# Moving the last chunk of batch 0 ahead of the second mean, at the start of a linear-attention and ELU-MLP kernel

## Chip, cores, metric

The kernel runs on one core of a Trainium2 chip. The metric is the device time of one execution, in microseconds, as the median over several executions of the same kernel.

## The reference

The work is a linear attention without softmax, a root-mean-square norm of each head's output, and a two-layer MLP with an ELU between the layers:

```python
# q, k, v: (8 batches, 8 heads, 576 rows, 64); g_norm: (64,)
kv  = einsum('bhsd,bhse->bhde', k, v)
out = einsum('bhsd,bhde->bhse', q, kv)
rms = sqrt(mean(out * out, axis=-1, keepdims=True) + 1e-6)
x   = (out / rms * g_norm)            # turned to (4608 tokens, 512)
h   = x @ w_in                        # w_in: (512, 2048)
g   = where(h > 0, h, exp(min(h, 0)) - 1)
y   = g @ w_out                       # w_out: (2048, 512)
```

Inputs and outputs are float32; the matmuls take bfloat16 operands.

## The kernel before

The 4608 tokens are worked on in nine tiles of 512 tokens. For each tile the kernel needs the normed attention output, turned so that the model dimension lies on the partitions (`xT[T]`, four chunks of 128 rows). Then the first MLP matmul (`h_ps`, sixteen blocks of 128 rows, done in pairs), the ELU on ScalarE and VectorE (giving `gT`), and the second matmul (`o_ps`). The instructions stand in an order written out by hand, and each engine works through its own in that order.

The change lies in the start, where tile 0 is made from batch 0. There nothing can be overlapped with an earlier tile, so batch 0 goes through in four chunks of two heads, numbered 0 to 3, worked on in the order 0, 2, 1, 3. For each chunk the steps are:

- `chunk_kv`: K^T V on TensorE (line 156), 18 matmuls of 64x64, and `chunk_kv_out`: VectorE copies it to SBUF as bfloat16 (line 112).
- `chunk_y`: q times K^T V, two matmuls of 64x64 by 512 columns (line 189), and `chunk_square`: ScalarE squares it (line 551).
- `mean_mm`: a matmul with a block matrix of 1/64 gives the mean of squares over each head, spread over its rows (line 199).
- `inv_t`, or its parts written out: ScalarE takes Ln of the mean plus 1e-6 and then Exp of minus half of it (lines 208 and 209, 627 and 636, 559 and 562). For chunks 1 and 3 the Exp is in two halves of 256 columns.
- `chunk_scale`: VectorE multiplies the product by the norm factor and by g, and writes one chunk of `xT[0]` (line 212).

`early(tiles, c)` (line 569) multiplies a finished chunk c of `xT[0]` with its part of `w_in` for the first six MLP blocks, so TensorE has 24 matmuls of 512 columns which can start as chunks get ready. `idle(n, ps)` (line 525) issues n matmuls on zeros whose result is never read. After the early matmuls the other ten blocks of tile 0 follow (`mm1`, line 382), then the second matmul `mm2_all` (line 403), with batch 1's attention between its parts.

K and V of the chunks 1 to 3, all of `w_in` and `w_out` and batch 1's inputs come through POOL's DMA queue in one fixed order: k and v of chunk 2, q of chunks 1 and 3, k and v of chunks 1 and 3, `w_in` for the first six blocks in four pieces by chunk (0, 2, 1, 3), the rest of `w_in` in three pieces, the first quarter of `w_out`, half of batch 1, two quarters of `w_out`, the other half of batch 1, and the last quarter.

PSUM is a second ordering force. Tags A and B are one pair of banks each; tags "m" and "x" are two single banks each, used in turn. A new tile of a tag waits until the last reader of the tile before it in the same bank is through. So the product of chunk 1 takes the bank of the mean of chunk 2, the product of chunk 3 takes the bank of the product of chunk 0, and `h_ps[1]` takes the banks of K^T V (tag B).

Of the kernel before, what the change touches and what calls it, by code (L numbers as in the profile page):

```python
# [16 lines left out]
def kernel(  # L17
# [16 lines left out]
    B, H, S, D = q.shape  # L34
# [8 lines left out]
    V, A, Q = nc.vector, nc.scalar, nc.gpsimd  # L43
# [64 lines left out]
    def copy_on(eng, out_, in_):  # L108
        if eng is nc.scalar:
            nc.scalar.copy(out_, in_)  # L110
        else:
            eng.tensor_copy(out=out_, in_=in_)  # L112
# [16 lines left out]
    def single(tag, name):  # L129
        pool = ps_x if tag == "x" else ps_m2  # L130
        return pool.tile([P, 512], FP32, name=name, tag=tag)

    def pair(tag, name):
        if tag in ("x", "m", "mx"):
            return [single(t, name) for t in (tag + tag)[:2]]
        return ps_m1.tile([P, 2, 512], FP32, name=name, tag=tag)
# [14 lines left out]
    def kv_mm(b, kv_ps, u, ls=range(2)):  # L151
        for j in range(RK):
            for s in range(2):
                rows = slice(s * 64, s * 64 + 64)
                for l in ls:
                    nc.tensor.matmul(  # L156
                        kv_ps[s][l * 64 : l * 64 + 64, u * 64 : u * 64 + 64],
                        lhsT=bf["k", b][rows, 2 * l + u, j, :],
                        rhs=bf["v", b][rows, 2 * l + u, j, :],
                        start=(j == 0),  # L160
                        stop=(j == RK - 1),
                    )
# [18 lines left out]
    def y_mm(T, u, ps, ls=range(2)):  # L181

        n = 0
        while n < 8:
            b, j = slot_of(T, n)
            m = min(8 - n, RK - j)
            for l in ls:
                for s in range(2):
                    nc.tensor.matmul(  # L189
                        ps[l][s * 64 : s * 64 + 64, n * 64 : (n + m) * 64],  # L190
                        lhsT=kv_of(b, l, u, s),
                        rhs=qT[b][l * 64 : l * 64 + 64, s, u, j : j + m, :],
                        start=True,
                        stop=True,
                    )
            n += m

    def mean_mm(sq, ps):
        nc.tensor.matmul(ps, lhsT=ones, rhs=sq, start=True, stop=True)  # L199
# [4 lines left out]
    def r_tile():  # L204
        return outp.tile([P, 2, G], FP32, name="rT", tag="o")
# [5 lines left out]
    def scale_t(T, ps, r, cs, cols=slice(0, 512)):  # L211
        nc.vector.scalar_tensor_tensor(  # L212
            out=xT[T][:, cs, cols], in0=ps, scalar=g_col, in1=r, op0=ALU.mult, op1=ALU.mult
        )
# [308 lines left out]
    def idle(n, ps):  # L523
        for _ in range(n):
            nc.tensor.matmul(ps, lhsT=zeros[:, 0:P], rhs=zeros, start=True, stop=True)
# [10 lines left out]
    def chunk_kv(kv_ps, c):  # L536
        kv_mm(0, [kv_ps[:, s, :] for s in range(2)], c % 2, (c // 2,))

    def chunk_kv_out(kv_ps, c, eng):
        rows, cols = slice(c // 2 * 64, c // 2 * 64 + 64), slice(c % 2 * 64, c % 2 * 64 + 64)  # L540
        copy_on(eng, kv_sb[rows, 0, c % 2], kv_ps[rows, :, cols])

    y_ps, sq0 = {}, {}

    def chunk_y(c, ps):
        y_ps[c] = ps
        y_mm(0, c % 2, {c // 2: ps}, (c // 2,))

    def chunk_square(c):
        sq0[c] = attp.tile([P, G], BF16, name="sq", tag="sq")  # L550
        nc.scalar.activation(sq0[c], y_ps[c], AF.Square)

    def chunk_scale(c, r, cols=slice(0, 512)):
        scale_t(0, y_ps[c][:, cols], r[:, cols], c, cols)
# [10 lines left out]
    def early(tiles, c):  # L565

        for i, a in tiles:
            h = h_ps[i]
            nc.tensor.matmul(  # L569
                h[a] if isinstance(h, list) else h[:, a, :],  # L570
                lhsT=w_in_sb[:, c, (2 * i + a) * P : (2 * i + a) * P + P],
                rhs=xT[0][:, c, :],
                start=(c == 0),
                stop=(c == KC - 1),
            )
# [4 lines left out]
    kv_ps = pair("B", "kv_ps")  # L580
# [23 lines left out]
    r = r_tile()  # L604
# [5 lines left out]
    inv_t(r[:, 1, :], mean)  # L610
    kv_ps = pair("B", "kv_ps")
    h_ps = [pair("A", "h_ps")]
    idle(2, h_ps[0][:, 0, :])
    chunk_kv(kv_ps, 1)
    chunk_kv_out(kv_ps, 1, V)
    idle(1, h_ps[0][:, 0, :])
    chunk_y(1, single("m", "y_ps"))
    chunk_square(1)
    chunk_scale(0, r[:, 0, :])
    idle(1, h_ps[0][:, 0, :])  # L620
    chunk_kv(kv_ps, 3)
    chunk_kv_out(kv_ps, 3, V)
    chunk_scale(2, r[:, 1, :])
    mean = single("m", "mean")
    mean_mm(sq0[1], mean)
    r = r_tile()
    nc.scalar.activation(r[:, 0, :], mean, AF.Ln, bias=eps_col)
    y3 = single("x", "y_ps")
    h_ps += [None, [single("x", "h_ps"), None]]
    chunk_y(3, y3)  # L630
    chunk_square(3)
    h_ps[1] = pair("B", "h_ps")
    early([(0, 0), (0, 1), (1, 0), (1, 1), (2, 0)], 0)
    for n in range(2):
        cols = slice(n * 256, n * 256 + 256)
        nc.scalar.activation(r[:, 0, cols], r[:, 0, cols], AF.Exp, scale=-0.5)
# [30 lines left out]
    for u in range(2):  # L667
# [4 lines left out]
        kv_ps = [single("x", "kv_ps") for _ in range(2)]  # L672
# [95 lines left out]
    for T in range(2, NT):  # L768
        at, early, late = {}, {}, {}
        if T + 1 < NT:  # L770
# [12 lines left out]
            early = {2: ("sum0", "inv0"), 4: ("sum1", "inv1"), 5: ("gain0",), 7: ("gain1",)}  # L783
            late = {0: ("kv",), 1: ("se0",), 2: ("mul0",), 3: ("se1",), 4: ("mul1", "ahead")}
        if T == 2:
            early = {2: ("sum0", "inv0"), 5: ("sum1", "inv1", "mul1"), 6: ("gain0",), 7: ("gain1",)}
# [45 lines left out]
```

## Time and profile before

| | |
|---|---|
| median of 4 executions | 285.78 us (285.60 to 285.99) |
| the profiled execution's own time | 285.60 us |
| its span, first to last instruction | 283.8 us |
| TensorE busy | 276.9 us (98% of the span) |
| VectorE busy | 165.9 us (58%) |
| ScalarE busy | 141.5 us (50%) |
| DMA, mean over the span | 139 GB/s |

The profile shows one execution. A row of its timeline has the start in microseconds from the span's start, the duration, the engine, the line of the kernel, the operation and its tiles, and in brackets how long the engine had been idle before it and what released it. PE is TensorE, PEld its weight loads, DVE VectorE, ACT ScalarE, POOL GpSimd. A row with "x2" stands for neighbouring instructions of one kind taken together. Matmuls are pipelined: one of 512 columns has a duration of about 0.38 us but the next can start 0.216 us after it.

### The profile page before, as it was taken

How to read it: one execution, taken by the hardware profiler on the slowest of the kernel's cores; microseconds unless marked ns; L12 is line 12 of the kernel's file. 1: busy time of each engine (PE TensorE's matmuls, PEld its weight loads, DVE VectorE, ACT ScalarE, POOL GpSimd, SP SyncE). 2: the span in 40 equal slices, each digit the busy share in tenths (PEclk: the TensorE clock that was granted, in tenths of full speed). 3: DMA queues.
4: the chain of work that ended last, by engine and by line, in shares of the span. 5: the costliest groups of instructions: out<-in, count | busy, mean ns of one | idle time of the engine just before them, and what ended most of it. 6: DMA issues, size and time to landing. Idle time of an engine off the chain costs nothing.

```text
span 283.8 us, 5154 instructions
## 1 busy us (share of the span) xinstructions
PE 276.9 (98%) x2124; PEld 129.1 (45%) x2124; DVE 165.9 (58%) x222; ACT 141.5 (50%) x209; POOL 49.5 (17%) x89
## 2 busy tenths in 40 slices
PE   7899999999999999999999999999999999999994
PEld 3444444444544444444444444444444444444443
DVE  2449532967478658655775478537873787344500
ACT  3778359594567355425542555245533553333320
POOL 7743303312313033034003210000000000000000
PEclk9999999999999999999999999999999999999999
DMA  7999999999999979789628961602150235020222
GB/s 208 195 204 206 206 260 240 195 297 144 163 266 108 164 194 232 85 192 263 147 29 177 264 156 40 164 14 74 39 111 0 74 39 111 0 76 0 74 74 75
DMA packets 50572, 39.46 MB, mean 139 GB/s; under 512 B 30965, under 2 KB 44021, under 8 KB 50549
## 3 DMA queue, kind: packets, MB, share of 16 engines
q0 software_dynamic: 15008, 21.30, 37.2%
q1 hardware_dynamic: 35136, 17.31, 30.1%
q10 hardware_dynamic: 404, 0.53, 0.5%
q8 instruction: 16, 0.26, 0.4%
q14 instruction: 8, 0.06, 0.1%
HBM read 36.70 MB, written 9.44 MB: 163 GB/s over the span
## 4 chain that ended last, share of the span: by engine, by line
PE 94%; DMA 3%; DVE 1%; ACT 0%; SPq 0%; issue 0%; DVEq 0%
PE o_ps L403 43%; PE h_ps L382 42%; DMA first_v<-in_v_dram 2%; PE at L250 2%; PE h_ps L569 2%; PE at L156 1%; PE kv_ps L156 1%; PE y_ps L189 1%; PE qt_ps L174 1%; PE mean L199 1%; DMA out_dram<-o_sb 1%; PE o_ps L440 1%; DVE gT L366 0%; ACT elu_e L350 0%; SPq L90 0%; DVE kv_sb L112 0%
## 5 line engine op out<-in xcount | busy, mean ns | idle before, releaser
L403 PE MATMUL o_ps<-w_out_sb,gT 128*128 128x512 bf16 x560 | 129.7, 379 | 0.0
L382 PE MATMUL h_ps<-xT,w_in_sb 128*128 128x512 bf16 (+1 forms) x560 | 128.0, 376 | 0.1
L350 ACT ACTIVATE elu_e<-h_ps 128x1024 bf16<-128x1024 f32 (+1 forms) x79 | 74.1, 952 | 89.0 <-PE h_ps L382 87.6
L403 PEld LDWEIGHTS <-gT 128*128 128x128 bf16 x560 | 54.3, 98 | 65.9 <-issue 0.9
L382 PEld LDWEIGHTS <-w_in_sb 128*128 128x128 bf16 x560 | 53.1, 98 | 61.4 <-issue 0.4
L366 DVE TENSOR_TENSOR gT<-elu_e,h_ps 128x1024 bf16<-128x1024 bf16 (+1 forms) x67 | 77.2, 1157 | 6.6
L362 DVE TENSOR_SCALAR elu_e<-elu_e 128x1024 bf16<-128x1024 bf16 x72 | 32.3, 449 | 64.7 <-ACT elu_e L350 64.6
L419 ACT COPY o_sb<-o_ps 128x512 f32<-128x512 f32 x32 | 18.4, 588 | 21.0 <-PE o_ps L403 20.3
L103 POOL CAST q_bf<-st_q 128x384 bf16<-128x384 f32 x36 | 18.3, 552 | 39.9 <-DMA st_q<-in_q_dram 39.9
L283 DVE TENSOR_REDUCE ss<-sq 128x16 f32<-128x1024 bf16 x14 | 17.1, 1218 | 5.7 <-ACT sq L277 5.5
L299 DVE TENSOR_TENSOR xs<-at,ss 128x1024 bf16<-128x1024 f32 x14 | 17.1, 1219 | 1.9 <-ACT ss L292 1.9
L277 ACT ACTIVATE sq<-at 128x1024 bf16<-128x1024 f32 x14 | 14.4, 1028 | 0.0
L212 DVE SCALAR_TENSOR_TENSOR xT<-y_ps,g_col,rT 128x512 bf16<-128x512 f32 (+1 forms) x10 | 6.2, 640 | 9.8 <-ACT rT L209 7.9
L339 POOL COPY gate<-qT 1x16 bf16<-1x16 bf16 x5 | 1.1, 213 | 57.7 <-DMA qT<-q_bf 57.7
L355 ACT ACTIVATE elu_h<-h_ps 128x1024 bf16<-128x1024 f32 (+1 forms) x12 | 9.3, 816 | 0.0
L156 PEld LDWEIGHTS <-k_bf 64*64 64x64 bf16 x576 | 6.4, 107 | 5.3 <-issue 5.3
L90 POOL DMA_DIRECT2D v_bf<-in_v_dram x11 | 7.7, 696 | 4.2 <-DMA w_in_sb<-in_moe_w_in_dram 2.0
L90 POOL DMA_DIRECT2D k_bf<-in_k_dram x11 | 7.8, 709 | 2.8 <-DMA w_in_sb<-in_moe_w_in_dram 2.1
L312 DVE TENSOR_SCALAR xT<-xT,g_col 128x1024 bf16<-128x1024 bf16 x14 | 6.7, 482 | 1.9 <-DMA xT<-xs 1.7
L366 DVE TENSOR_TENSOR gT<-elu_e,elu_h 128x1024 bf16<-128x1024 bf16 x9 | 6.7, 742 | 0.8
L112 DVE COPY o_sb<-o_ps 128x256 f32<-128x256 f32 x1 | 0.4, 426 | 11.5 <-DMA out_dram<-o_sb 11.5
L250 PEld LDWEIGHTS <-qT 64*128 64x128 bf16 (+1 forms) x248 | 4.3, 97 | 6.1 <-issue 5.9
(57 smaller groups left out, 101.3 us busy)
## 6 DMA issues: line engine op xcount, KB each, us to landing
st_q<-in_q_dram POOLq DMA_DIRECT2D x6, 1152.0 KB, 8.2
out_dram<-o_sb SPq DMA_DIRECT2D x24, 256.0 KB, 3.4
k_bf<-in_k_dram POOLq DMA_DIRECT2D x6, 576.0 KB, 10.4
v_bf<-in_v_dram POOLq DMA_DIRECT2D x6, 576.0 KB, 12.6
out_dram<-o_sb SPq DMA_DIRECT2D x19, 128.0 KB, 2.5
w_out_sb<-in_moe_w_out_dram POOLq DMA_DIRECT2D x4, 512.0 KB, 14.9
w_in_sb<-in_moe_w_in_dram POOLq DMA_DIRECT2D x2, 512.0 KB, 11.0
q_bf<-in_q_dram POOLq DMA_DIRECT2D x3, 288.0 KB, 13.4
```

What stands on the lines that cost most here:

```text
L90: eng.dma_start(out=dst.rearrange("p m j d -> p m (j d)"), in_=in_[:, ms, :])
L103: nc.gpsimd.tensor_copy(out=bf["q", b][:, u, js], in_=raw[b][:, u::2, js, :].rearrange("p l j d -> p j l d"),)
L156: nc.tensor.matmul(kv_ps[s][l * 64 : l * 64 + 64, u * 64 : u * 64 + 64], lhsT=bf["k", b][rows, 2 * l + u, j, :], rhs=bf["v", b][rows, 2 * ...
L277: nc.scalar.activation(sq, st["se", h], AF.Square)
L283: nc.vector.reduce_sum(out=ss, in_=st.pop(("sq", h)).rearrange("p l (m e) -> p (l m) e", e=D), axis=AX.X,)
L299: nc.vector.tensor_tensor(out=st["xs"][:, 2 * h : 2 * h + 2, :].rearrange("p i (l m e) -> p l i m e", l=2, e=D), in0=se_ps.rearrange("p l ...
L350: nc.scalar.activation(e[:, lo:hi, :], h, AF.Exp)
L362: nc.vector.tensor_scalar(out=e, in0=e, scalar1=1.0, scalar2=1.0, op0=ALU.min, op1=ALU.subtract)
L366: nc.vector.tensor_tensor(out=gT[T][:, 2 * i + lo : 2 * i + hi, :], in0=e[:, lo:hi, :], in1=h, op=ALU.add if relu else ALU.max,)
L382: nc.tensor.matmul((ps[a] if isinstance(ps, list) else ps[:, a, :])[:, cols], lhsT=w_in_sb[:, c, f * P : f * P + P], rhs=xT[T][:, c, cols] ...
L403: nc.tensor.matmul(o_ps[T, j], lhsT=gT[T][:, f, j * P : j * P + P], rhs=w_out_sb[:, f, :], start=(f == 0), stop=(f == FC - 1),)
L419: nc.scalar.copy(o_sb[T, half][:, j % 2, :], o_ps[T, j])
```

## The change

Chunk 3's K^T V, its copy, its product and its square are moved forward. K^T V of chunk 1 and its copy now come directly after the mean of chunk 2, the two fillers after them; then the scale of chunk 0, then chunk 3's K^T V and copy, then the product and square of chunk 1, one filler, and chunk 3's product and square. Of the four fillers in this stretch three are left. The scale of chunk 2 follows chunk 3's square. Two of the five early matmuls of chunk 0 now come ahead of the mean of chunk 1, the other three after it. ScalarE's order was square 1, Ln 1, square 3, Exp 1, Ln 3, Exp 3; it is now square 1, square 3, Ln 1, Exp 1, Ln 3, Exp 3.

```diff
     kv_ps = pair("B", "kv_ps")
     h_ps = [pair("A", "h_ps")]
-    idle(2, h_ps[0][:, 0, :])
     chunk_kv(kv_ps, 1)
     chunk_kv_out(kv_ps, 1, V)
-    idle(1, h_ps[0][:, 0, :])
+    idle(2, h_ps[0][:, 0, :])
+    chunk_scale(0, r[:, 0, :])
+    chunk_kv(kv_ps, 3)
+    chunk_kv_out(kv_ps, 3, V)
     chunk_y(1, single("m", "y_ps"))
     chunk_square(1)
-    chunk_scale(0, r[:, 0, :])
     idle(1, h_ps[0][:, 0, :])
-    chunk_kv(kv_ps, 3)
-    chunk_kv_out(kv_ps, 3, V)
+    y3 = single("x", "y_ps")
+    h_ps += [None, [single("x", "h_ps"), None]]
+    chunk_y(3, y3)
+    chunk_square(3)
     chunk_scale(2, r[:, 1, :])
+    h_ps[1] = pair("B", "h_ps")
+    early([(0, 0), (0, 1)], 0)
     mean = single("m", "mean")
     mean_mm(sq0[1], mean)
     r = r_tile()
     nc.scalar.activation(r[:, 0, :], mean, AF.Ln, bias=eps_col)
-    y3 = single("x", "y_ps")
-    h_ps += [None, [single("x", "h_ps"), None]]
-    chunk_y(3, y3)
-    chunk_square(3)
-    h_ps[1] = pair("B", "h_ps")
-    early([(0, 0), (0, 1), (1, 0), (1, 1), (2, 0)], 0)
+    early([(1, 0), (1, 1), (2, 0)], 0)
     for n in range(2):
         cols = slice(n * 256, n * 256 + 256)
         nc.scalar.activation(r[:, 0, cols], r[:, 0, cols], AF.Exp, scale=-0.5)
```

## The prediction

> **What bounds the kernel now.** I read the page's chain first, then the chain in order of time from 8 to 24 us, then the timeline of that stretch engine by engine, and last the times at which the loads land. The chain says what the end hangs on:
>
> ```profile
> PE 94%; DMA 3%; DVE 1%; ACT 0%; SPq 0%; issue 0%; DVEq 0%
> ```
>
> TensorE (PE) carries the span, so only PE time counts. From 27.9 us to 57 us the chain in order of time has PE rows alone, and after that it goes on as dense matmul blocks (1.73 us for 8 of 512 columns, 0.216 us each). Whatever PE gains before 28 us is thus kept unless something it waits for comes no earlier. The edit lies between 10.7 and 18.2 us. There the timeline, all engines together (start, duration, engine, line), reads:
>
> ```profile
> 4.96 0.58 POOL L90 DMA_DIRECT2D v_bf<-in_v_dram  x1
> ...
> 5.49 0.59 POOL L116 DMA_DIRECT2D w_in_sb<-in_moe_w_in_dram  x1
> ...
> 8.32 0.38 PE L156 MATMUL kv_ps<-v_bf,k_bf 64*64 64x64 bf16 x13 [0.38 <-DVE kv_sb L112]
> ...
> 8.51 0.40 PE L189 MATMUL y_ps<-qT,kv_sb 64*64 64x512 bf16 x1
> ...
> 10.67 0.39 PE L199 MATMUL mean<-sq,ones 128*128 128x512 bf16 x1
> ...
> 11.47 0.47 PE L156 MATMUL kv_ps<-v_bf,k_bf 64*64 64x64 bf16 x18
> ...
> 12.17 0.63 ACT L209 ACTIVATE rT<-rT 128x512 f32<-128x512 f32 x1
> ...
> 12.32 0.40 PE L189 MATMUL y_ps<-qT,kv_sb 64*64 64x512 bf16 x2
> ...
> 13.41 0.38 PE L199 MATMUL mean<-sq,ones 128*128 128x512 bf16 x1
> ...
> 13.83 0.69 ACT L627 ACTIVATE rT<-mean,eps_col 128x512 f32<-128x512 f32 x1 [0.47 <-PE mean L199]
> ...
> 13.84 0.40 PE L189 MATMUL y_ps<-qT,kv_sb 64*64 64x512 bf16 x2
> ...
> 14.89 0.72 ACT L636 ACTIVATE rT<-rT 128x256 f32<-128x256 f32 x2
> ...
> 16.11 0.69 ACT L559 ACTIVATE rT<-mean,eps_col 128x512 f32<-128x512 f32 x1 [0.50 <-PE mean L199]
> ...
> 17.28 0.88 DVE L212 SCALAR_TENSOR_TENSOR xT<-y_ps,g_col,rT 128x256 bf16<-128x256 f32 x2 [1.06 <-ACT rT L562]
> 17.67 0.77 POOL L122 DMA_DIRECT2D w_out_sb<-in_moe_w_out_dram  x1 [1.54 <-DMA w_in_sb<-in_moe_w_in_dram]
> 18.21 1.18 PEld L569 LDWEIGHTS <-w_in_sb 128*128 128x128 bf16 x6 [0.26 <-issue]
> ...
> 33.24 1.90 PE L403 MATMUL o_ps<-w_out_sb,gT 128*128 128x512 bf16 x8
> ```
>
> The reader should see three things. ScalarE stops twice for a mean (0.47 us at 13.83, 0.50 us at 16.11). The last norm's product, two halves from 17.28 to 18.16, is what PE waits for at 18.21: the last early matmuls (chunk 3) cannot start sooner. And PE has short holes before that, at 12.32 and 13.84, both for a copy of K^T V by VectorE.
>
> The loads have to be read too. The queries of single tiles give issue to landing of each POOL load; added to the issue time above: v of chunk 3 lands at 4.96 + 7.1 = 12.06 us, the first w_in block (chunk 0) at 5.49 + 7.7 = 13.2, chunk 3 of w_in at 9.44 + 7.9 = 17.34, w_in columns 8 to 11 at about 21.05, and the second w_out block like this:
>
> ```profile
> DMA to landing us min/median/max: 15.3/15.3/15.3
> ```
>
> that is 17.67 + 15.3 = 32.97 us. Its first user is the row at 33.24 (mm2 with f = 4). So this load is hidden by only 0.27 us.
>
> **The change part by part.** The durations are of one profiled execution: span 283.8, its own time 285.60, so 1.8 us lie outside the span. It is the quickest of the four; the median is 285.78. I make the sum in the span and take it off the median.
>
> *The dropped idle.* Of four filler matmuls in this stretch three are left: 0.216 us of PE less, on the path only where PE is not waiting.
>
> *K^T V of chunk 1 first.* It now follows the mean of chunk 2 directly: 10.67 plus 0.31 (a full matmul followed by 64x64 ones: 12.66 to 12.98 shows 0.32) gives 10.98 instead of 11.47. Its copy follows VectorE's qT copy (to 11.47) and ends at 11.77; the scale of chunk 0 runs at 11.70 to 12.43 instead of 12.19 to 12.92.
>
> *Chunk 3 ahead of y1.* The two idles end at about 11.75, then K^T V of chunk 3 is the next in PE's order and its v is not there before 12.06: a new wait of 0.3 us, starting at 12.09. Queued behind it on PE: y1, y3, all means and early matmuls. y1 sat at 12.32. The nearest row for the pair is chunk 2, K^T V at 8.32 with y0 at 8.51[...]: so y1 at 12.28 to 12.37. If they did not overlap, it would be 12.48. I take the first, as it is the same pair of shapes. The square of chunk 1 stays at 12.79, behind the Exp row at 12.17. The copy of chunk 3 comes 0.51 after its matmuls (as in the rows at 8.32 and 8.83): 12.60 to 12.88; the scale of chunk 0 ahead of it on VectorE is over at 12.43, so it costs nothing. It would, if the Exp of chunk 0 ended later than about 11.8 (it ends at 11.56). y3: 13.00 instead of 13.84; its square 13.43 to 14.02.
>
> *Two early matmuls ahead of the second mean.* They start 0.33 after y3, at 13.33; the w_in block landed at 13.2, so 0.1 us is the whole slack there. The mean of chunk 1 goes from 13.41 to 13.76, its Ln (0.42 later, as 13.41 to 13.83) to 14.18. That is 0.35 us later than now. The Exp does not get later: now a square stands between Ln and Exp; afterwards the Exp follows 0.72 us behind its Ln (10.21 to 10.93), at 14.90 against 14.89. Scale of chunk 1: 15.35 to 16.23, no gain.
>
> *The last norm.* PE counts on from 13.76: mean, three early, two of chunk 2, then the last mean at 15.06 instead of 15.69. Its Ln would be ready at 15.48; ScalarE is in the two Exp halves until about 15.55. Exp at 16.27, scale 16.72 to 17.60 instead of 17.28 to 18.16: 0.56 us sooner. PE meanwhile: three of chunk 2 until 15.92, then the five of chunk 1 want xT of 16.23: a wait of 0.35 us that is not there now (they sit at 16.56 now). 16.27 plus 7 x 0.216 is 17.78 for the first chunk 3 matmul instead of 18.21. **Gain at that place 0.43 us** (0.29 without the overlap of y1; 0.56 if chunk 1 made no wait).
>
> *Carrying on.* The first Exp of the ELU moves from 18.84 to 18.41 and pair A is free at 21.22 instead of 21.65; the load for it landed at 21.05. So PE arrives at the row of 33.24 at 32.81. There the second w_out block is the next late thing: 32.97 and some 0.05 us for the start. **0.19 us are given back; what is left is about 0.22.** The moved steps issue no DMA, and POOL's and SP's queues are in the same order, so this landing stays where it is: POOL's loads wait only for older loads, and the 16 engines are full (207 GB/s from 18.2 to 33.2). After it the nearest is the last w_out block: 27.86 + 14.5 = 42.36, wanted at 42.81, and 0.22 sooner is still later than it.
>
> *The clock.* The profile grants 1.00 throughout, but the first fillers run at half speed (loads 0.43 us apart from 1.59 to 4.15, later matmuls 0.216). The Trainium skill, page "TensorE: Matmul & The Clock Gate", section "Part 1: The HAM clock gate", says that the clock halves after an idle window of about 3.4 us; fewer fillers and two new holes of 0.35 us speak against the change by it. The row that stands against this is of the busy time by stretches (stretch, its length, PE's share and matmuls first):
>
> ```profile
> 7.00:8.00 1.00, 0.47 (x18) 0.46 (x18) 0.35 (x2) 0.40 (x1) 0.54 (x1) 1.00 1.21 206
> ```
>
> PE was busy for 0.47 of that us, for 0.68 of the four us from 5 to 9 (the mean of that view's four rows), and matmuls went on at 0.216 after it. By the rows the change costs 0 here; by the rule, if one window did pass at half clock, 8 matmuls would fill its 3.4 us, which is 1.7 us of work: an estimated loss of 1.7 us. I take 0.
>
> Sum: 0.43 - 0.19 = 0.2 to 0.25, so 285.78 - 0.23 = 285.55.
>
> **The rivals.**
> 1. *The load does not hold it* (it lands earlier in other executions, or the semaphore was seen at once). Then 0.43 to 0.65 remain: 285.1 to 285.35. For: DMA times vary. Against: the stream is bandwidth-bound and in order.
> 2. *The change does not do what it says*: ScalarE pauses just the same, since v of chunk 3 (12.06) or the w_in block (0.1 us of slack) is a little later, and what was gained is lost at 13.3. Time 285.7 to 285.95. For: every 0.1 us of v's landing goes 1:1 into y3, Ln and the last scale. 0.4 us late takes all of it.
> 3. *Slower: the half clock.* Place: after the hole at 11.75 to 12.09 and the one at 15.9 to 16.27. Price 1.7 us less the gain of 0.4, so about +1.3: 287.1; a partial window 286.4. It decides when a window counts as idle at some 70 to 80% busy; the trace shows that 47 to 68% did not.
>
> **How the numbers follow.** Forecast 0.55, rival 1 0.14, rival 2 0.18, rival 3 and whatever else delays PE 0.13. A measurement of this kernel tells about 0.2% (0.57 us) from no change. The forecast and rival 2 lie wholly within that; of rival 1 about half passes it. Hence faster 0.08, same 0.79, slower 0.13. The forecast's own range is 285.3 to 285.8 (the gain from 0 to 0.45); rival 1 takes the lower end to 285.1, and the upper end at 286.3 takes in rival 2 and the scatter of the medians, and leaves out the half clock.
>
> **What would show it.** Right: y3 at 13.0, Ln of chunk 1 near 14.2 without a pause of over 0.2 us before it, the last scale ending near 17.6, first chunk 3 matmul near 17.8, and PE idle about 0.2 us before its mm2 block near 33.0, released by the w_out load. Wrong: that block starting before 32.9 (rival 1), the chunk 3 matmuls at 18.1 or later (rival 2), matmuls 0.427 us apart between 11 and 19 us (rival 3), or a PE wait after 33 us that is not there now.

## The result, and the profile after

The changed kernel takes 285.26 us (median; 284.88 to 286.69) against 285.85 us for the kernel before, measured beside it. The two medians differ by 0.59 us. The ratio of the times, which comes with an interval and is used below, is 0.9985 (0.9978 to 0.9992, at 95%). That is 0.43 us faster, with an interval of 0.23 to 0.63 us. The forecast was 0.23 us. A repeat later gave 0.9996 (0.9983 to 1.0009). Weighted by the inverse squares of their intervals the two give about 0.36 us, so the size is known only as "a few tenths".

The profiled execution took 284.97 us with a span of 283.2 us, 0.63 us less than the 285.60 of the profile before. The positions below add up to that (us from the span's start):

| place | before | after | shift |
|---|---|---|---|
| mean of chunk 2 | 10.67 | 10.94 | +0.27 |
| first early matmul | 14.17 | 13.47 | -0.70 |
| first matmul of the other ten blocks, `mm1` (L382) | 19.72 | 19.45 | -0.27 |
| mm2 block with f = 4 (L403) | 33.24 | 32.97 | -0.27 |
| last VectorE copy, counted from the first L440 matmul | 4.11 | 3.75 | -0.36 |

So between these two profiles the time came from two places: 0.27 us in the changed stage, kept to the end, and 0.36 us at the last copy, where nothing was edited. The 0.27 us are a difference of two things: the stage itself is 0.54 us shorter (8.51 us from the mean of chunk 2 to `mm1`, against 9.05), and it began 0.27 us later. The stage in the timeline of after, all engines together (start, duration, engine, line, operation):

```profile
10.94 0.39 PE L199 MATMUL mean<-sq,ones 128*128 128x512 bf16 x1
11.26 0.47 PE L156 MATMUL kv_ps<-v_bf,k_bf 64*64 64x64 bf16 x18
...
12.20 0.37 PE L156 MATMUL kv_ps<-v_bf,k_bf 64*64 64x64 bf16 x12
...
13.14 0.40 PE L189 MATMUL y_ps<-qT,kv_sb 64*64 64x512 bf16 x2
...
13.47 0.61 PE L569 MATMUL h_ps<-xT,w_in_sb 128*128 128x512 bf16 x2
...
13.92 0.38 PE L199 MATMUL mean<-sq,ones 128*128 128x512 bf16 x1
...
14.33 0.69 ACT L632 ACTIVATE rT<-mean,eps_col 128x512 f32<-128x512 f32 x1 [0.15 <-PE mean L199]
...
15.05 0.72 ACT L636 ACTIVATE rT<-rT 128x256 f32<-128x256 f32 x2
...
15.68 0.67 ACT L559 ACTIVATE rT<-mean,eps_col 128x512 f32<-128x512 f32 x1
...
16.43 3.18 PE L569 MATMUL h_ps<-xT,w_in_sb 128*128 128x512 bf16 x14 [0.19 <-DVE xT L212]
...
19.45 9.05 PE L382 MATMUL h_ps<-xT,w_in_sb 128*128 128x512 bf16 x40
```

ScalarE's two pauses of 0.47 and 0.50 us have shrunk to one of 0.15 us ahead of the Ln at 14.33. From that Ln to the one at 15.68 it does not stop. PE has the new wait before chunk 1's early matmuls (16.43).

The end, last copy of each kernel's timeline, before and then after:

```profile
280.08 0.43 DVE L112 COPY o_sb<-o_ps 128x256 f32<-128x256 f32 x1 [11.47 <-DMA out_dram<-o_sb]
```

```profile
279.45 0.42 DVE L112 COPY o_sb<-o_ps 128x256 f32<-128x256 f32 x1 [11.10 <-PE o_ps L440]
```

The same copy, of the same size, has an idle time 0.37 us shorter, and another releaser. In before the first L440 matmul is at 275.97, in after at 275.70.

### The profile page after: what moved, and what is told of

Same layout as the page of the kernel before. It is cut to its first block, busy times and chain, and to the rows that moved or that the text cites. A ratio compares the mean times of both kernels' runs of the same rounds, so it can differ in the third digit from the quotient of the medians.

```text
span 283.2 us, 5154 instructions
## 1 busy us (share of the span) xinstructions
PE 277.2 (98%) x2123; PEld 129.3 (46%) x2123; DVE 164.6 (58%) x222; ACT 141.4 (50%) x209; POOL 50.0 (18%) x89
## 4 chain that ended last, share of the span: by engine, by line
PE 96%; DVE 2%; ACT 1%; issue 0%; DVEq 0%
PE o_ps L403 43%; PE h_ps L382 42%; PE at L250 2%; PE kv_ps L525 2%; PE at L156 1%; PE o_ps L440 1%; PE qt_ps L174 1%; PE h_ps L569 1%; PE kv_ps L156 1%; PE mean L199 1%; PE y_ps L189 1%; DVE gT L366 0%; ACT elu_e L350 0%; PE h_ps L525 0%; DVE xT L212 0%; ACT rT L632 0%
## 5 line engine op out<-in xcount | busy, mean ns | idle before, releaser
L403 PE MATMUL o_ps<-w_out_sb,gT 128*128 128x512 bf16 x560 | 129.7, 379 | 0.0
L382 PE MATMUL h_ps<-xT,w_in_sb 128*128 128x512 bf16 (+1 forms) x560 | 128.0, 376 | 0.1
L403 PEld LDWEIGHTS <-gT 128*128 128x128 bf16 x560 | 54.4, 98 | 65.9 <-issue 0.9
L382 PEld LDWEIGHTS <-w_in_sb 128*128 128x128 bf16 x560 | 53.2, 98 | 61.3 <-issue 0.4
L362 DVE TENSOR_SCALAR elu_e<-elu_e 128x1024 bf16<-128x1024 bf16 x72 | 31.3, 435 | 65.1 <-ACT elu_e L350 65.1
L103 POOL CAST q_bf<-st_q 128x384 bf16<-128x384 f32 x36 | 18.9, 567 | 38.5 <-DMA st_q<-in_q_dram 33.1
```

Source lines behind the costliest of these rows:

```text
L103: nc.gpsimd.tensor_copy(out=bf["q", b][:, u, js], in_=raw[b][:, u::2, js, :].rearrange("p l j d -> p j l d"),)
L362: nc.vector.tensor_scalar(out=e, in0=e, scalar1=1.0, scalar2=1.0, op0=ALU.min, op1=ALU.subtract)
L382: nc.tensor.matmul((ps[a] if isinstance(ps, list) else ps[:, a, :])[:, cols], lhsT=w_in_sb[:, c, f * P : f * P + P], rhs=xT[T][:, c, cols] ...
L403: nc.tensor.matmul(o_ps[T, j], lhsT=gT[T][:, f, j * P : j * P + P], rhs=w_out_sb[:, f, :], start=(f == 0), stop=(f == FC - 1),)
```

## The experiments

Theories. T1: the stage is held by landings (v of chunk 3, then the first `w_in` block), so its new end is fixed by the loads. T2: it is held by work on the engines, and the gain would be the same everywhere. T3: part of the gain has nothing to do with the order in the stage. Each ratio is against executions of the kernel before on the same chip.

**The kernel before, and the changed kernel, once more.** No edit.

> The kernel before, unchanged, as a second look. Stretch S, from the mean of chunk 2 on TensorE to the first matmul of line 382, was 9.05 us in the first profile (10.67 to 19.72); both theories expect 9.0 to 9.1 again, since S leaves out the start, which lay 0.27 us apart in the two profiles. The second w_out block is wanted 13.52 us after that. What is open is the end: VectorE's last copy came 0.45 us after TensorE's last matmul before and 0.09 us after. If that belongs to the kernel, 0.45 again; if it is chance, either value. Time within 0.3 us of the kernel before.

> The changed kernel again. S was 8.51 us (10.94 to 19.45) where the forecast had 8.62. Theory 1 (the second w_out block's landing takes back what S gains beyond 0.22 us): a wait of 0.1 to 0.2 us ahead of the mm2 block in an execution whose start is early (mean of chunk 2 at 10.67). Theory 2 (no such wait; all of S is kept): that block 13.52 us after the first line 382 matmul whatever the start. If the last copy's 0.09 us belongs to the change, 0.09 again. Time 0.4 to 0.6 us under the kernel before by theory 2, 0.2 by theory 1.

Ratios 1.0003 (0.9992 to 1.0013) and 0.9996 (0.9983 to 1.0009). In the profiles `mm1` stands at 20.00 in before and at 19.47 in after, with the mean of chunk 2 at 10.96 and 10.80. Before's `mm1` follows the mean of chunk 2: 9.05 us behind it in the first profile and 9.04 in this. After's does not: 8.51 and 8.67 us behind it, at the same place. The start itself moves between executions, since PE's first matmuls run at half speed (fillers 0.43 us apart, later 0.216), and the profiles differ in when that turns. In before it turned between 4.15 and 4.4 us, with the eighth of the ten fillers; in after all ten were slow, and so were the transposes of q up to 6.5 us.

**K^T V of chunk 1 first, nothing else.** It tells whether this part alone brings anything.

```diff
-    idle(2, h_ps[0][:, 0, :])
     chunk_kv(kv_ps, 1)
     chunk_kv_out(kv_ps, 1, V)
-    idle(1, h_ps[0][:, 0, :])
+    idle(2, h_ps[0][:, 0, :])
     chunk_y(1, single("m", "y_ps"))
```

> The kernel before with one part of the change: K^T V of chunk 1 directly behind the mean of chunk 2, the two fillers after it, the third filler of this place dropped; chunk 3 stays where it was. If the early start of chunk 1 and the dropped filler were the source, S falls to about 8.6. By the forecast's sum chunk 1's product then still waits for the bank of the mean of chunk 2 (free at 12.13) and starts at 12.2 to 12.3, so S is 8.95 to 9.05 and the time within 0.2 us of the kernel before.

0.9998 (0.9990 to 1.0006); `mm1` at 19.66 with the mean of chunk 2 at 10.60, 9.06 us behind it as in before. That looks like the expected answer, but the timeline (PE and its weight loads) shows another cause:

```profile
13.89 1.19 PEld L569 LDWEIGHTS <-w_in_sb 128*128 128x128 bf16 x7 [0.23 <-issue]
14.12 1.46 PE L569 MATMUL h_ps<-xT,w_in_sb 128*128 128x512 bf16 x6 [0.16 <-issue]
...
16.63 3.20 PE L569 MATMUL h_ps<-xT,w_in_sb 128*128 128x512 bf16 x14 [0.18 <-DMA w_in_sb<-in_moe_w_in_dram]
```

Seven weight loads stand against six matmuls: the record of the first early matmul is missing, and it began at 13.9. That is 3.3 us behind the mean of chunk 2, where before has 3.5. The last norm's product also came sooner, at 17.00, 6.40 us behind that mean against 6.61. What held `mm1` is the piece of `w_in` for chunk 1, which landed 8.7 us after its issue; in the other profiles where it is loaded in the same place it took 7.1 to 7.5. From the last product's end (17.88) and the 1.56 us that follow it in before (18.16 to 19.72) one can estimate 19.44 for `mm1` without that landing, 8.84 us behind the mean. So this part alone may bring some 0.2 us; neither the profile nor the ratio shows whether it does, and that the gain needs chunk 3 moved too is not shown.

One thing the expectation had wrong: the product of chunk 1 started at 11.85, while the Ln that reads the mean of chunk 2 ran from 11.39 to 12.06. So it does not wait for the bank of that mean, although the description of the kernel ahead of the prediction says so.

**One early matmul ahead of the mean instead of two.**

```diff
-    early([(0, 0), (0, 1)], 0)
+    early([(0, 0)], 0)
     mean = single("m", "mean")
...
-    early([(1, 0), (1, 1), (2, 0)], 0)
+    early([(0, 1), (1, 0), (1, 1), (2, 0)], 0)
```

> The changed kernel with one early matmul of chunk 0 ahead of the mean of chunk 1 in place of two. In the changed kernel TensorE stops 0.35 us for the scale of chunk 1, which follows from the Ln at 14.33. With the mean 0.216 us sooner the Ln starts when ScalarE is through with the square of chunk 3, about 0.15 us sooner; the stop shrinks to about 0.2 us and S to about 8.36. Theory 2: the time falls 0.15 us too. Theory 1: the gain is taken back at the second w_out block, whose slack in the changed kernel's profile was 0.22 us in an execution with a late start and is less in one with an early start.

0.9975 (0.9964 to 0.9985), 0.71 us faster than before. PE's early matmuls and then ScalarE's Ln, in the timeline:

```profile
13.45 0.39 PE L569 MATMUL h_ps<-xT,w_in_sb 128*128 128x512 bf16 x1
...
15.40 4.12 PE L569 MATMUL h_ps<-xT,w_in_sb 128*128 128x512 bf16 x17
```

```profile
14.09 0.69 ACT L632 ACTIVATE rT<-mean,eps_col 128x512 f32<-128x512 f32 x1
```

The Ln comes 0.24 us sooner than in after (14.33), PE's wait at 16.4 no longer has a row of its own (one row of 17 from 15.40; at 0.216 us each they would take 3.67 us, and `mm1` follows after 3.95, so 0.28 us of waiting is left in it), and `mm1` stands at 19.35, 0.10 to 0.12 us sooner than in the two profiles of after. Behind the stage this is lost again in the profile: the last block's first matmul (L440) is at 275.78, in after at 275.70. So the 0.84 us between the medians of this kernel and of the repeat of after are not accounted for by the stage. The quickest executions of the two differ by 0.08 us (284.82 and 284.90).

**One more VectorE instruction in before, one fewer in after.** The changed kernel has one more semaphore instruction on VectorE than before (the traces record 325 instructions against 324; the 327 and 326 below count two more in each). If it is this that moves the last copy, a memset added to before should move it as well, and one taken from after (given to POOL) should undo it.

```diff
 # before, plus one
     nc.vector.memset(ones, 0.0)
+    spare = const.tile([P, 1], FP32, name="spare")
+    nc.vector.memset(spare, 0.0)
 # after, minus one
     for c in (0, 2, 1, 3):
         load_w_in(slice(0, 6), slice(c, c + 1))
+        if c == 0:
+            nc.gpsimd.memset(eps_col, 1e-6)
...
-    nc.vector.memset(eps_col, 1e-6)
```

> The kernel before with one instruction more on VectorE, a memset of a 128x1 tile that nothing reads, at the start where VectorE is idle. The three profiles in which VectorE's last copy came 4.11 us after the first matmul of line 440 all have 326 instructions on VectorE, and an instruction-queue DMA at that copy; the three with 3.75 us have 327, and that DMA 4 us sooner. Theory 3 (the end's 0.36 us is the place where VectorE fetches instructions, moved by one extra semaphore instruction in the changed kernel): 3.75 us, S unchanged at 9.05, time 0.36 us under the kernel before. Rival (the end belongs to the new order): 4.11 us and no change in time.

> The changed kernel with one instruction less on VectorE: the memset of eps_col is done by POOL while it waits for a DMA slot. The order around chunk 3 is the changed one. Theory 3: the last copy comes 4.11 us after the first matmul of line 440 again, and the time is 0.36 us over the changed kernel, so only the stage's own 0.2 to 0.3 us under the kernel before is left. Rival: 3.75 us, time as the changed kernel. First line 382 matmul at 19.45 to 19.5 by both.

The last copy in the timelines of the two kernels, before plus one and then after minus one:

```profile
280.12 0.42 DVE L112 COPY o_sb<-o_ps 128x256 f32<-128x256 f32 x1 [11.10 <-PE o_ps L440]
```

```profile
281.81 0.43 DVE L112 COPY o_sb<-o_ps 128x256 f32<-128x256 f32 x1 [11.45 <-DMA out_dram<-o_sb]
```

The end changed sides as T3 said: 3.75 us behind the first L440 matmul with the added instruction, 4.10 with one taken away. In all fourteen profiles of this case it is 4.10 to 4.12 in five (before, its repeat, chunk 1 first, after minus one, and before with other loads) and 3.74 to 3.75 in the other nine. The times don't confirm it: ratios 0.9996 (0.9988 to 1.0005) and 0.9993 (0.9981 to 1.0005). For before plus one a step of 0.36 us would be 0.9987, just outside its interval; its profile lost 0.30 us elsewhere, between 45 and 72 us, and whether the other executions did is not known. After minus one was expected at 0.9990 to 0.9993, which fits, but the ratios of after (0.9985 and 0.9996) lie on both sides. The quickest executions don't settle it either: 285.10 and then 285.48 us for before plus one, against 285.39 and 285.42 for before beside it; 285.16 and 285.30 for after minus one, where after had 284.88 and 284.89.

After minus one also began close to the time that the forecast had assumed (mean of chunk 2 at 10.56; 10.67 was assumed). So its PE timeline is the cleanest check of the forecast's positions:

```profile
12.09 0.38 PE L156 MATMUL kv_ps<-v_bf,k_bf 64*64 64x64 bf16 x13 [0.20 <-DMA v_bf<-in_v_dram]
...
13.00 0.40 PE L189 MATMUL y_ps<-qT,kv_sb 64*64 64x512 bf16 x2
...
13.49 0.60 PE L570 MATMUL h_ps<-xT,w_in_sb 128*128 128x512 bf16 x2
```

K^T V of chunk 3 at 12.09 and its product at 13.00 are the forecast's numbers to the hundredth. The early matmuls are 0.16 us late (13.33 was forecast), and the chain of waits up to there, in order of time (start, length, what), says for what:

```profile
5.46 7.98 DMA w_in_sb<-in_moe_w_in_dram
13.44 0.05 issue
```

**After without the two fillers** between K^T V of chunk 1 and that of chunk 3: the test of the half clock, and of whether work or a landing holds chunk 3.

```diff
     chunk_kv_out(kv_ps, 1, V)
-    idle(2, h_ps[0][:, 0, :])
     chunk_scale(0, r[:, 0, :])
```

> The changed kernel without the two fillers between K^T V of chunk 1 and of chunk 3. If v of chunk 3 sets the start of its K^T V (it landed at 12.06 to 12.16, K^T V began at 12.20 and 12.25), that start stays within 0.1 us of 12.2 and the first line 382 matmul stays at 19.4 to 19.5 although TensorE has 0.43 us less to do; no time is gained. If TensorE's own order sets it, K^T V starts at 11.7 and everything up to line 382 comes 0.4 us sooner. If the two fillers keep the clock up, matmuls of 512 columns come 0.43 us apart after 12 us and the time is over 1 us longer.

0.9977 (0.9964 to 0.9990), 0.66 us faster than before. PE's timeline:

```profile
11.98 0.38 PE L156 MATMUL kv_ps<-v_bf,k_bf 64*64 64x64 bf16 x13 [0.61 <-DMA v_bf<-in_v_dram]
...
13.43 0.60 PE L569 MATMUL h_ps<-xT,w_in_sb 128*128 128x512 bf16 x2
```

PE now stands still for 0.61 us, and the release is the landing of v. Chunk 3 starts 0.11 us sooner than in after minus one, which had begun at nearly the same time, and the early matmuls still start at 13.43: the second landing (the first `w_in` block, at 13.38) takes the gain, and `mm1` stands at 19.44. The last 14 early matmuls take 3.05 us to `mm1`, 0.218 each; no clock was lost. The quickest execution, 284.88 us, is that of after too.

**128 KB more ahead of the second `w_out` block** in POOL's queue.

```diff
+    spare_w = const.tile([P, 1, 512], BF16, name="spare_w")
+    nc.gpsimd.dma_start(out=spare_w, in_=moe_w_out.rearrange("(c p) f -> p c f", p=P)[:, 0:1, :])
     for s in (1, 2):
         load_w_out(s)
```

> The changed kernel with an extra 128 KB load into a tile that nothing reads, ahead of the second w_out block in POOL's queue: by the 207 GB/s of this stretch that block lands 0.63 us later. If the block was just hidden, as the forecast's sum has it (slack 0 to 0.25 us), TensorE waits 0.4 to 0.65 us ahead of its mm2 block (13.9 to 14.2 us after the first line 382 matmul, against 13.52) and the time rises by as much. If the load has more room than the landing times say, nothing changes.

0.9999 (0.9987 to 1.0012), and in PE's timeline a wait that no other profile has:

```profile
33.45 1.24 PE L403 MATMUL o_ps<-w_out_sb,gT 128*128 128x512 bf16 x5 [0.32 <-DMA w_out_sb<-in_moe_w_out_dram]
```

From `mm1` to this block it is 13.90 us instead of 13.52: 0.38 us lost, just under what was expected. The forecast's statement that this load is barely hidden holds: of the 0.63 us that it was made late, about 0.25 were hidden.

**Chunk 3 with the v of chunk 1**, on top of the kernel without fillers: is it v that holds it?

```diff
-        kv_mm(0, [kv_ps[:, s, :] for s in range(2)], c % 2, (c // 2,))
+        kv_mm(0, [kv_ps[:, s, :] for s in range(2)], c % 2, (c // 2,), 1 if c == 3 else None)
```

> The changed kernel without the two fillers, with chunk 3's K^T V taken from v of chunk 1, so that part of the result is another; all loads stay. It tells which load holds the changed stage. In the changed kernels seen so far the first early matmul began at 13.43 to 13.57 whether chunk 3's product was at 12.90 or 13.24. If v of chunk 3 (landing near 12.1) holds the stage, K^T V of chunk 3 starts near 11.4, its product near 12.4, the first early matmul near 12.8 and the first line 382 matmul near 19.1. If the first w_in block (landing near 13.2 to 13.45) holds it, the first early matmul stays at 13.4 to 13.5 and the first line 382 matmul at 19.4 to 19.5.

0.9976 (0.9962 to 0.9990), no better than without the edit. The profile can't tell which landing holds an early start, since this execution began late (mean of chunk 2 at 11.13). Chunk 3 then waited for VectorE's copy of chunk 1's K^T V, to 12.30; the first early matmul (its record is missing, its weight load is at 13.61) followed chunk 3's product by 0.33 us, half a microsecond behind the landing of the first `w_in` block (13.1). So a late start is held by neither landing but by the work itself, as T2 has it.

**Loads split.** On the kernel with one early matmul: the second `w_out` block in two halves; then the first `w_in` block split too; then both splits in before.

```diff
 # w_out: all three kernels
-    for s in (1, 2):
-        load_w_out(s)
+    for fs in (slice(4, 6), slice(6, 8)):
+        nc.gpsimd.dma_start(
+            out=w_out_sb[:, fs, :], in_=moe_w_out.rearrange("(c p) f -> p c f", p=P)[:, fs, :]
+        )
+    load_w_out(2)
 # w_in: the second and third kernel
-    for c in (0, 2, 1, 3):
+    load_w_in(slice(0, 2), slice(0, 1))
+    load_w_in(slice(2, 6), slice(0, 1))
+    for c in (2, 1, 3):
```

> One early matmul ahead of the mean of chunk 1, and the second w_out block loaded in two halves, so that f = 4 and 5, which are wanted first, land about 1.2 us sooner. One early matmul alone gave 19.35 for the first line 382 matmul and 13.59 us from there to the mm2 block. If the load was what stretched that, it is 13.52 now and the mm2 block begins at 32.85 to 32.9; time 0.05 to 0.1 us under that kernel, 0.75 under the kernel before. If something else stretched it, 13.59 stays.

> As the last, and the first w_in block also in two parts, blocks 0 and 1 first, which the first two early matmuls use. If the first w_in block holds the changed stage, the first early matmul now follows the product of chunk 3 by 0.33 us, at 13.2 to 13.4, the stop before the matmuls of chunk 1 shrinks, and the first line 382 matmul comes at 19.1 to 19.25 when the start is early; time 0.1 to 0.25 us under the kernel with the w_out block split alone. If v of chunk 3 or the norms on ScalarE hold it, no change from that kernel.

> The kernel before, order untouched, with both loads split in the same way. In it the first early matmul starts at 14.17, 0.9 us after its load, and the second w_out block has 0.27 us of room, so by every theory nothing moves: S 9.05, 13.52 us to the mm2 block, 4.11 us at the end, time within 0.2 us of the kernel before. A gain here would mean that the split loads themselves, and not the order together with them, bring it.

Ratios 0.9984 (0.9970 to 0.9999), 1.0011 (0.9991 to 1.0030) and 0.9996 (0.9983 to 1.0008): no gain over 0.9975. With `w_out` split, the way from `mm1` to the mm2 block is 13.52 us again (13.59 without), which fits the load as the cause of the 0.07 us there; it is one profile each. With `w_in` split too, the first early matmul follows the product of chunk 3 by 0.33 us as expected, but at 13.54, no sooner, because that product came only at 13.21. And a later piece is now late, in PE's timeline:

```profile
16.59 3.20 PE L574 MATMUL h_ps<-xT,w_in_sb 128*128 128x512 bf16 x14 [0.28 <-DMA w_in_sb<-in_moe_w_in_dram]
```

## Why the prediction was right, and where it was not

**The direction and the mechanism held.** ScalarE's pauses went, the mean of chunk 1 came later (13.92; 13.76 forecast), and the last norm came sooner (its product ends at 17.71; 18.16 before, 17.60 forecast). In the profile that began near the assumed time the positions held up to chunk 3's product. From the first early matmul on the sum was right: 5.96 us to `mm1` by the forecast, 5.97 to 6.01 in the six profiles with two early matmuls ahead of the mean.

**The gain of the stage is partly luck.** Taken over four profiles each, `mm1` stands at 19.90 with the old order (before, its repeat, before plus one, before with split loads: 19.72, 20.00, 19.82, 20.05) and at 19.48 with the new (19.45, 19.47, 19.46, 19.55, the last with the later `w_out`): 0.42 us, against 0.43 forecast. But the two orders are anchored differently. The old one follows PE's start: 9.04 to 9.06 us behind the mean of chunk 2, wherever that falls from 10.60 to 11.00. The new one follows it only when it is late: 8.51 us behind it from 10.94 (after) and from 11.04 (with the later `w_out`). With an earlier start the landings hold it, and `mm1` stands at 19.46 to 19.47 from 10.56 as from 10.80. So from the forecast's own start of 10.67 the gain is about 0.26 us, from a late one 0.54. The forecast, which had the new wait for v in its sum, is between the two.

**The mis-sized term was the start of the early matmuls, 13.33.** They started at 13.43 to 13.62 in the new order, and all of the 0.16 us by which `mm1` of after (19.45) is behind the forecast's 19.29 (19.72 less 0.43) lies ahead of them. What was late differs. "0.1 us is the whole slack there" failed in the two profiles with the earliest starts: the first `w_in` block landed at 13.44 (7.98 us after its issue, in the chain of waits above) and 13.38, where 13.2 was taken. That is rival 2's mechanism, 0.16 us of the 0.4 us at which it would have taken all. In the repeat of after it was v of chunk 3, landed at 12.16 instead of 12.06. In after's first profile it was neither: the start was 0.27 us late, and the early matmul follows the product of chunk 3 by 0.33 us (13.14 to 13.47), as forecast.

**"0.19 us are given back" was not seen.** The way from `mm1` to the mm2 block is 13.52 us in before and in after, 13.53 in the repeat, 13.59 and 13.61 in the two best kernels: 0 to 0.09 us. Two reasons. The stage arrived at 32.97 rather than 32.81, which is exactly when the load was expected; and the load itself moved, to 32.75 in after (issued at 17.45, 15.3 us), 33.0 in the repeat, 32.87 in the kernel with one early matmul. The two errors of 0.16 and 0.19 us cancelled: 0.43 - 0.19 was forecast, 0.27 - 0 was measured in the profile.

**What the forecast did not have is the end.** No step spoke of the last copy, and 0.36 of the 0.63 us between the two profiles lies there. The median, 285.26, lies in the range of rival 1 and not near the 285.55 of the sum; in the profiles it is this end, and not the load of rival 1, that makes the difference. "The chain says what the end hangs on" was read as a matter of PE alone; the overview's line with the last copy and its 11.5 us of idle time, released by a DMA and not by the matmuls, was not asked about.

**The rivals.** Rival 1 (the load does not hold) is in part what happened at 33 us, but the medians do not rest on it. Rival 2 happened at a small size. Rival 3, the half clock: the kernel without the two fillers left PE idle for 0.61 us, and its matmuls stayed at 0.218 us. The hole of 1.83 us that after minus one has at 71 us (below) changed nothing either: the 16 matmuls of 256 columns behind it take 1.92 us, and 1.91 in after, where there is no hole. So the value taken from the rows, 0, held. The rule that was weighed against it (the Trainium skill, page "TensorE: Matmul & The Clock Gate", section "Part 1: The HAM clock gate": an idle window of about 3.4 us halves the clock) is not tested by a hole that short; no run here shows one of 3.4 us.

**What the medians can carry.** From one execution to the next a place far from the edit moves more than the edit does. At 71 us PE wants the turned `xT` of tile 2, made by a DMA transpose. Timeline of after, SP and VectorE, and then of after minus one, with PE:

```profile
61.32 8.09 SPq L306 DMA_TRANSPOSE xT<-xs  x4
...
69.39 0.49 DVE L312 TENSOR_SCALAR xT<-xT,g_col 128x1024 bf16<-128x1024 bf16 x1 [0.24 <-DMA xT<-xs]
```

```profile
61.33 8.06 SPq L306 DMA_TRANSPOSE xT<-xs  x4
...
72.18 0.49 DVE L312 TENSOR_SCALAR xT<-xT,g_col 128x1024 bf16<-128x1024 bf16 x1 [2.79 <-DMA xT<-xs]
72.77 0.49 PE L382 MATMUL h_ps<-xT,w_in_sb 128*128 128x256 bf16 x3 [1.83 <-DVE xT L312]
```

Issued at the same time, it was there 8.1 us later in one and 10.85 us later in the other, and that cost PE 2.0 us. Before lost nothing here in its first profile and 0.6 us in its repeat, after nothing and 0.47, the kernel with both splits 1.9. The best two kernels lost nothing here in their profiles. So a ratio of 0.9975 against one of 0.9985 or 0.9996 may be this scatter, which so few executions do not average out. The profiles' positions settled where the time went. Of the times, those of the order with one early matmul, with and without the split `w_out`, and of the two kernels without the fillers have intervals below 1; the changed kernel itself has one in its first measurement and none in its repeat.

## What to carry to other kernels

Before summing a stage's gain, ask what each end of it is anchored to. Work that follows the engine's start and work that follows a landing drift apart between executions; the later of the two sets the end, and a gain between such anchors has a width that one profile doesn't show. A load with 0.1 us of slack should be costed as late by as much as its landings vary: here the first `w_in` block landed from 13.1 to 13.4 us. When a control run comes out as expected, look whether it was held by what the expectation names. When an unedited place has moved between two profiles, compare distances inside each (here from the last block's first matmul to the last copy) ahead of explaining all of the difference by the edit.

## What the runs showed of the hardware

The last VectorE copy starts 0.36 us later or sooner by whether VectorE's trace has 324 or 325 instructions. In the view of line 112, the row of its queue gives the two semaphore instructions ahead of the copy (shortest, median and longest in ns, and first and last start in us). Before, after, before plus one, after minus one:

```profile
L112 DVEq EVENT_SEMAPHORE  x2: 50/1824/3597, 276.0 to 276.1; - x2
```

```profile
L112 DVEq EVENT_SEMAPHORE  x2: 50/1646/3243, 275.7 to 276.2; - x2
```

```profile
L112 DVEq EVENT_SEMAPHORE  x2: 50/1645/3240, 276.4 to 276.8; - x2
```

```profile
L112 DVEq EVENT_SEMAPHORE  x2: 50/1826/3602, 277.7 to 277.8; - x2
```

The first of the two takes 0.05 us. In before the second follows it at 0.1 us, waits for the matmuls until 276.1 + 3.6 = 279.7, and the copy starts 0.4 us after that, at 280.08. In after the second follows only at 0.5 us, waits until 276.2 + 3.24 = 279.44, and the copy starts at once, at 279.45. The kernel with one more instruction looks like after, the one with one fewer like before. So there is a stop of about 0.4 us at a fixed place in VectorE's program, and one more instruction ahead moves it from behind the long wait, where it costs its whole length, to in front of it, where it costs nothing. A transfer of the instruction queue (q14 in the profile) goes with it: 0.7 us behind the start of the copy in before and in after minus one (280.7 and 282.5), and 0.7 us behind the second semaphore's start in the other two (276.8 and 277.5), so in all four behind the instruction that the stop held up. That the stop is the change to the next block of fetched instructions is inferred from this, and was not tested further. The gain is shown in the traces; the times of the two kernels don't show it clear of the scatter.

The releaser that the profile names for the late copy, an output DMA, is not the cause. In before it was issued at 278.3. The same transfer was issued at 278.05 in after and could not have landed before 279.95 (1.9 us is the shortest landing of that tile), but the copy there began at 279.45.
